# Sliding-window attention beside an S4 convolution: items of 512 queries by eight heads, square half tiles of the PE array, masks added by matmuls, the DFT split 64 by 32, and the order of the source

## The chip, the cores and the metric

The kernel runs on one core of a Trainium2 chip. A core has five engines that work side by side, each through its own instructions in order: PE (TensorE, matmuls; its weight loads are shown as PEld), DVE (VectorE), ACT (ScalarE), POOL (GpSimd) and SP (SyncE, which here only issues transfers). The metric is device time in microseconds of one execution; smaller is better.

PE is an array of 128 rows (the contraction) by 128 columns (the partitions of the output). A matmul may use only a part of it: 64 rows by 64 columns is called a half tile here, and four of them fill the array.

## The reference

Two independent parts share the launch, and their outputs stand side by side in a [1, 2048, 1152] tensor.

```python
# part A: attention, 32 heads of 18, each query sees the last 256 keys
qkv = (x @ wqkv).reshape(B, S, 3, H, Dh).transpose(2, 0, 3, 1, 4)   # S=2048, D=576
scores = einsum("bhqd,bhkd->bhqk", q, k) * Dh ** -0.5
mask = (i - j >= 0) & (i - j < 256)
p = softmax(where(mask, scores, -1e9))
a = einsum("bhqk,bhkd->bhqd", p, v).transpose(0, 2, 1, 3).reshape(B, S, D) @ wo
# part B: S4, 128 states per channel
K = einsum("dn,dnl,dn->dl", C, exp(dt * A * l), dt * B).real          # l = 0..2047
y = irfft(rfft(u, 4096) * rfft(K, 4096))[:2048] + u * Dskip
```

## The kernel before

The work stands in four stages.

*Projection, tables, first DFT of u.* `proj` (L153) splits x and wqkv into f16 high and low halves and forms q, k and v with 14 matmuls per output tile (`mm14`, L143); q and k go to DRAM as `qd`, v as `vd`. `tables` builds the S4 kernel K from exponentials, sines and cosines: products on POOL (L350), contraction over the 128 states in PE's four column groups (L388). `s1_u` (L433 and around) does the first step of a DFT of u. The three are generators, taken in turn by `merge` in fixed proportions; the framework's scheduler then orders the instructions of each engine by its own estimate of what is ready.

*First DFT of K* (`s1_k`): 48 matmuls, evacuated by ACT and DVE in turn (`evac`, L111), written to DRAM as `gk` in rows of 144 f32.

*The loop over 16 items.* An item is 1024 queries (half of them all) of 4 heads.
- `gmax` finds each query's largest score. The item's q is copied into a block-diagonal form of 4 heads by 32 queries (L580, DVE); a matmul gives the scores of 32 queries of 4 heads with their 288 keys (L593), a second adds the mask (L596), DVE takes the maximum (L602). The maxima are transposed, scaled to f16 and sent into a row of the stacked Q by four small transfers in POOL's queue (L613), so that the second score matmul subtracts them.
- `att_chunk` makes transposed scores of 128 keys by up to 384 queries from stacked f16 halves (L634), takes exponentials into SBUF (L636, ACT), cuts the two triangles out with `affine_select` on POOL (L645), and multiplies with V and a column of ones (L652), one head to each column group of 32.
- `norm` sends the sums through DRAM and back (den, rd, rb, all in POOL's queue), multiplies, splits the output in f16 halves, and stores it as `od`.
- `conv` runs beside it: 16 rounds of second DFT of x and K (L464), complex products on DVE (L486 to L495), inverse (L497), a store as `h`; then 16 rounds of the last inverse step (L517), an addition of u x Dskip (L513, L519) and the store of the output.
- `wo` is the output projection (again `mm14`); `wo_load` (L685) fetches and splits its weights through one tile named raw, in two rounds of four loads.

PSUM's eight banks are given out by use: two for the maxima's S, two for the scores ST, one for po, three for everything else (fps). `merge` mixes item i's `att_unit` (weight 23), the next item's `gmax` (17), `conv` (7) and from item 9 on `wo` (3), and the scheduler orders the rest, so that for instance wo_load's work lies beside the end of the projection.

*The end*: what is left of conv's last step, and the output projection of the second half.

## Time and profile before

| | |
|---|---|
| median of 3 runs | 1373.83 us (1372.09 to 1378.88) |
| span of the profiled execution, first to last instruction | 1366.8 us |
| the profiled execution's own time | not listed apart from its span; the median lies 7.0 us above that |
| busy: PE, DVE, ACT, POOL | 74%, 55%, 44%, 40% |
| granted clock of PE, mean | 0.828 |
| moved by transfers | 162.34 MB, 119 GB/s on average |

A row of groups reads: line of the code, engine, operation, output<-input by the program's names, their shapes, how many; behind the bar the busy time in us and the mean ns of one; behind the next bar the time that the engine sat idle just before them, and who ended that idle time. A row of the timeline reads: start in us, length in us, engine, line, operation, tiles, shape and count, and in brackets the idle time before it. An f32 matmul is recorded as two. PE's records include the way through the array, so that two may overlap; "issue" is time in which the engine waited for nothing that the profile shows. The clock is a share of full speed.

### The profile page before, as it was taken

How to read it: one execution, taken by the hardware profiler on the slowest of the kernel's cores; microseconds unless marked ns; L12 is line 12 of the kernel's file. 1: busy time of each engine (PE TensorE's matmuls, PEld its weight loads, DVE VectorE, ACT ScalarE, POOL GpSimd, SP SyncE). 2: the span in 40 equal slices, each digit the busy share in tenths (PEclk: the TensorE clock that was granted, in tenths of full speed). 3: DMA queues.
4: the chain of work that ended last, by engine and by line, in shares of the span. 5: the costliest groups of instructions: out<-in, count | busy, mean ns of one | idle time of the engine just before them, and what ended most of it. 6: DMA issues, size and time to landing. Idle time of an engine off the chain costs nothing.

```text
span 1366.8 us, 25524 instructions
## 1 busy us (share of the span) xinstructions
PE 1009.0 (74%) x10314; PEld 535.1 (39%) x10314; DVE 755.2 (55%) x1229; ACT 599.5 (44%) x879; POOL 549.1 (40%) x700
## 2 busy tenths in 40 slices
PE   1548898798889864876797789667888896666338
PEld 1224464464455532333343334333444453222116
DVE  4797667777753254566766677544555765411210
ACT  2867687687783320432343234422443352233002
POOL 0024343454450260244543354333534454576640
PEclk8659999999999986788888888757999997776559
DMA  9563142133125668144433444225344423434673
GB/s 269 141 181 103 34 116 75 54 75 98 50 56 153 168 179 229 52 128 113 125 117 107 127 125 146 84 65 143 87 114 137 140 75 109 105 88 118 160 177 130
DMA packets 155541, 162.34 MB, mean 119 GB/s; under 512 B 34752, under 2 KB 128512, under 8 KB 155232
## 3 DMA queue, kind: packets, MB, share of 16 engines
q1 hardware_dynamic: 138768, 128.65, 33.9%
q0 software_dynamic: 15152, 28.08, 7.2%
q10 hardware_dynamic: 1504, 3.99, 1.0%
q8 instruction: 81, 1.33, 0.4%
q14 instruction: 36, 0.29, 0.1%
HBM read 103.11 MB, written 57.15 MB: 117 GB/s over the span
## 4 chain that ended last, share of the span: by engine, by line
PE 43%; DVE 22%; DMA 14%; ACT 9%; issue 6%; POOL 5%; SPq 2%; ACTq 0%; DVEq 0%; POOLq 0%
PE po L652 7%; PE ST L634 6%; PE fps L464 5%; PE S L593 5%; PE pp L151 5%; DVE m L602 4%; DMA Q<-m 4%; PE fps L151 4%; ACT P L636 3%; PE fps L497 3%; PE kp L388 2%; PE pp L431 2%; DMA den<-osb 2%; DMA gk<-g 2%; DVE Qbd L580 2%
## 5 line engine op out<-in xcount | busy, mean ns | idle before, releaser
L636 ACT ACTIVATE P<-ST,esc 128x1024 f32<-128x1024 f32 (+1 forms) x192 | 203.5, 1060 | 270.3 <-PE ST L634 242.6
L602 DVE TENSOR_REDUCE m<-S 128x2 f32<-128x576 f32 x224 | 168.7, 753 | 163.1 <-PE S L596 161.4
L645 POOL TENSOR_SCALAR_AFFINE_SELECT P<-P 128x512 f32<-128x512 f32 x240 | 159.7, 695 | 199.5 <-ACT P L636 189.2
L350 POOL TENSOR_TENSOR m<-A,tr 128x1024 f32<-128x1024 f32 x72 | 149.5, 2098 | 193.5 <-PE kp L388 143.9
L593 PE MATMUL S<-kh,Qbd 96*128 96x288 f16 (+7 forms) x512 | 135.4, 323 | 87.4 <-DVE m L602 55.3
L634 PE MATMUL ST<-Q,K 96*128 96x384 f16 (+2 forms) x704 | 141.3, 320 | 65.4 <-ACT P L636 38.1
L652 PE MATMUL po<-P,V 128*32 128x256 f32 (+2 forms) x1408 | 132.9, 458 | 14.3 <-POOL P L645 13.1
L634 PEld LDWEIGHTS <-K 96*128 96x128 f16 x704 | 64.8, 108 | 150.5 <-issue 132.3
L388 PE MATMUL kp<-Q,m 128*32 128x64 f32 x4608 | 87.6, 229 | 27.5 <-DVE Q L371 10.5
L388 PEld LDWEIGHTS kp<-Q,m 128*32 128x32 f32 x4608 | 74.6, 115 | 55.6 <-issue 41.8
L593 PEld LDWEIGHTS <-Qbd 96*128 96x128 f16 x512 | 56.3, 111 | 97.1 <-issue 38.3
L596 PE MATMUL S<-bias,idb 128*128 128x64 bf16 x448 | 92.0, 216 | 0.0
L431 PE MATMUL pp<-ut,w 128*128 128x288 f32 x128 | 51.4, 526 | 42.2 <-DMA ut<-in_u_dram 24.9
L652 PEld LDWEIGHTS po<-P,V 128*32 128x32 f32 x1408 | 41.4, 122 | 82.1 <-issue 42.9
L596 PEld LDWEIGHTS <-idb 128*128 128x128 bf16 x448 | 47.9, 108 | 62.3 <-issue 59.3
L464 PE MATMUL fps<-tx,w 128*64 128x288 f32 x256 | 66.1, 456 | 0.0
L497 PE MATMUL fps<-Y,i 128*128 128x288 f32 x128 | 56.1, 537 | 11.1 <-DVE Y L495 6.3
L464 PE MATMUL fps<-tk,w 128*64 128x288 f32 x256 | 61.4, 430 | 0.4 <-DVE t L487 0.4
L517 PE MATMUL fps<-ho,i 128*64 128x288 f32 x128 | 29.7, 593 | 39.7 <-DMA ho<-h 33.3
L519 DVE TENSOR_TENSOR tk<-fps,tx 128x288 f32<-128x288 f32 x32 | 14.4, 457 | 73.6 <-PE fps L517 65.6
L114 ACT ACTIVATE X<-fps 128x288 f32<-128x288 f32 x64 | 25.8, 409 | 66.5 <-PE fps L464 62.1
L114 ACT ACTIVATE g<-pp 128x288 f32<-128x288 f32 (+1 forms) x84 | 34.5, 446 | 46.1 <-PE pp L431 25.3
(160 smaller groups left out, 1918.8 us busy)
## 6 DMA issues: line engine op xcount, KB each, us to landing
gx<-g SPq DMA_DIRECT2D x32, 288.0 KB
qd<-qst SPq DMA_DIRECT2D x36, 256.0 KB
gk<-g SPq DMA_DIRECT2D x16, 576.0 KB
tx<-gx SPq DMA_DIRECT2D x16, 576.0 KB
tk<-gk SPq DMA_DIRECT2D x16, 576.0 KB
h<-ho POOLq DMA_DIRECT2D x16, 576.0 KB, 3.6
ho<-h SPq DMA_DIRECT2D x64, 144.0 KB
raw<-in_xT_dram SPq DMA_DIRECT2D x16, 512.0 KB
```

Source lines behind the costliest of these rows:

```text
L151: self.nc.tensor.matmul(ps, u, v, start=(i == 0), stop=(i == len(ops) - 1))
L350: self.nc.gpsimd.tensor_tensor(m, A[:, ch, a0:a0 + 8].unsqueeze(3).to_broadcast(sh), tr[:, ch, part, 0:8].unsqueeze(2).to_broadcast(sh), o ...
L388: nc.tensor.matmul(kp[32 * st:32 * st + 32, c % 2 * JJ2 + j, :], m[:, ch, a0:a0 + 32], Q[:, ch, term % 2, :], start=(term == 0), stop=(ter ...
L464: nc.tensor.matmul(ps[64 * par:64 * par + 64, :288], w2[:, par, 64 * part:64 * part + 64], t[:, 2 * hs:2 * hs + 2, par, :], start=True, st ...
L497: nc.tensor.matmul(ps[:, :288], i1[:, par, :], Y, start=True, stop=True)
L593: nc.tensor.matmul(ps[:, u, :n[u]], bdt[:, t].rearrange("p j q -> p (j q)"), kh[:, k0:k1], start=True, stop=False, skip_group_check=True)
L596: nc.tensor.matmul(ps[:, u, :288].rearrange("p (a b) -> p a b", b=32)[:, 0:9:8], self.idb, self.bias, start=False, stop=True, skip_group_c ...
L602: nc.vector.tensor_reduce(m[:, 2 * sp:2 * sp + 2], ps[:, :, :n[0]], axis=AX.X, op=OP.max)
L634: nc.tensor.matmul(ps[:, u, o:o + n], d["K"][:, j, k0:k0 + 128], d["Q"][:, j, q0:q0 + n], start=True, stop=True, skip_group_check=True)
L636: nc.scalar.activation(pt[:, 2 * jp:2 * jp + 2, lo:hi], ps[:, :, lo:hi], AF.Exp, scale=self.esc)
L645: nc.gpsimd.affine_select(v, v, pattern=[[0, 4], [sg, 128]], compare_op=OP.is_ge, fill=0.0, base=-1 if far else 0, channel_multiplier=-sg)
L652: nc.tensor.matmul(po[32 * j:32 * j + 32, t0 * 128:t1 * 128], d["V"][:, kb * 76 + 19 * j:kb * 76 + 19 * j + 32], P[off // 512][:, j, o:o + ...
```

## The change

*Items.* An item is 512 queries of 8 heads: chunk c of four, octet o of four. The eight heads are four pairs; the two heads of a pair lie in partitions 0 to 63 and 64 to 127 of Q and K, each with its 54 rows of f16 halves. Q, K and V come from DRAM in the layout of the item (`qq`, `kk`, `k0`, `vd`), with each head's queries in a row. Three sets of Q and K are kept, and `load` fetches two items ahead.

*Half tiles.* The maxima (`smax`) and the scores (`att`) are made by four matmuls of 64 rows by 64 columns at a time, two heads of two pairs, into two banks: head r of pair-half b writes partitions 64 (r ^ b) and on of bank b. Blocks are 64 keys by up to 320 queries, so that less lies outside the window. P times V uses tiles of 64 rows by 32 columns, eight at a time. The block-diagonal copy of Q is gone.

*Masks.* POOL's affine_select is gone. Four further matmuls per piece, identity by a table of 0 and -3e38, add the mask to the scores in PSUM before the exponential.

*DFT.* 2048 is split into 64 by 32 where it was 32 by 64. Tiles in the first step have 64 rows (u) or 32 rows (K), in the second 64 rows by 32 columns, in the inverse 32 rows by 64 columns. There are 8 rounds of 3 thirds of the channels; ACT evacuates the spectrum of x, DVE multiplies it with that of K in PSUM by two wide products, POOL forms the sums Y. Dskip is added to K's first tap, so that u isn't read a second time. What goes to DRAM is written in rows of 2304 or 4608 bytes.

*PSUM and order.* In the loop three pairs of banks, "ring", serve maxima, scores, DFT and output projection in turn, and the fourth pair is po. The scheduler is off there (`manual_schedule`): each engine's instructions stand in the order of the source, written out as 16 items of five steps. `norm` is a generator that goes one part a step; its transfers, the maxima's and h's move from POOL's queue to SP's, so that SP issues all of them. `wo_load` stands behind the fifth step of the first item, `wo` gets a step from item 5 on and works on a chunk of 512 queries once its four items are normalised.

The diff, cut ("..." stands for lines left out):

```diff
-HQ = 1024
-HK = HQ + 256
+CQ = 512
+CK = 768
...
+def s1_u(self):
...
+    for ch in range(16):
+        ut = self.p["s1u"].tile([128, D], F32, name="ut")
+        for r in range(2):
+            nc.sync.dma_start(ut[64 * r:64 * r + 64], uv[:, (16 * r + ch) * D:(16 * r + ch + 1) * D])
...
+        for k in range(2):
+            ps = [self.p["pps"].tile([128, 512], F32, name="pp")[:, :288] for _ in range(2)]
+            for r in range(2):
+                nc.tensor.matmul(ps[r], self.wu[64 * r:64 * r + 64], ut[64 * r:64 * r + 64, 288 * k:288 * k + 288],
+                                 start=True, stop=True)
+            for r in range(2):
...
+def s1_k(self):
...
+    for n in range(16):
...
+            for h in range(2):
+                for u in range(2):
+                    s = 2 * q + u
+                    b = 32 * h + 2 * n
+                    nc.tensor.matmul(ps[:, u, :288], self.wk[32 * s:32 * s + 32, h],
+                                     self.K[32 * s:32 * s + 32, b:b + 2].rearrange("p l j -> p (l j)"),
+                                     start=(h == 0), stop=(h == 1), skip_group_check=True)
...
+        nc.sync.dma_start(gv[:, 2 * n * D:2 * n * D + 2 * D], st.rearrange("p l s j -> p (l s j)"))
+        yield
+def slot(self):
+    return self.p["ring"].tile([128, 2, 512], F32, name="ring")
...
+def spectra(self, t, ch):
...
+    px, pk = self.slot(), self.slot()
+    for x, ps in ((tx, px), (tk, pk)):
+        for i in range(2):
+            for q in range(2):
+                for s in range(2):
+                    for r in range(2):
+                        b = 2 * q + (r ^ s)
+                        o = (2 * s + q) * 64 + 32 * i
+                        nc.tensor.matmul(ps[32 * b:32 * b + 32, s, 192 * i:192 * i + 192],
+                                         w2[64 * r:64 * r + 64, o:o + 32],
+                                         x[64 * r:64 * r + 64, 2 * s + q, 192 * ch:192 * ch + 192],
+                                         start=(i == 0), stop=True, skip_group_check=True)
+    v = lambda z: z[:, :, :384].rearrange("p s (i j) -> p s i j", i=2)
+    X = fy.tile([128, 2, 2, 192], F32, name="X")
...
+    nc.scalar.activation(X, v(px), AF.Copy)
...
+    tt(t1, X, v(pk)[:, :, 0:1].to_broadcast(sh), op=OP.mult)
+    tt(t2, X, v(pk)[:, :, 1:2].to_broadcast(sh), op=OP.mult)
...
+    nc.gpsimd.tensor_tensor(Y[:, 0], t1[:, :, 0], t2[:, :, 1], op=OP.subtract)
+    nc.gpsimd.tensor_tensor(Y[:, 1], t1[:, :, 1], t2[:, :, 0], op=OP.add)
+    return Y
+def inverse(self, t, ch, Y):
...
+    ps = self.slot()
+    for s in range(2):
+        for i in range(2):
+            for b in range(4):
+                o = (2 * s + i) * 64
+                nc.tensor.matmul(ps[64 * (b % 2):64 * (b % 2) + 64, b // 2, 192 * s:192 * s + 192],
+                                 i1[32 * b:32 * b + 32, o:o + 64], Y[32 * b:32 * b + 32, i, s],
+                                 start=(s == 0 and i == 0), stop=(i == 1), skip_group_check=True)
+    nc.scalar.activation(self.ho[:, :, :, 192 * ch:192 * ch + 192].rearrange("p s b j -> p b s j"),
+                         ps[:, :, :384].rearrange("p b (s j) -> p b s j", s=2), AF.Copy)
...
+def conv(self):
...
+    for t in range(8):
+        for ch in range(3):
+            if ch == 1 and t < 7:
+                self.conv_load(t + 1)
+            Y = self.spectra(t, ch)
+            yield
+            if late is not None:
+                self.inverse(*late)
+            late = (t, ch, Y)
+            yield
...
+def smax(self, i):
...
+    for qb in range(8):
+        k0 = max(64 * qb, 256 if c == 0 else 0)
+        k1 = 64 * qb + 320
+        n = k1 - k0
+        full = n == 320
+        for pp in range(2):
+            ps = self.slot()
+            for b in range(2):
+                for r in range(2):
+                    z = 64 * (r ^ b)
+                    rr = slice(64 * r, 64 * r + 54)
+                    nc.tensor.matmul(ps[z:z + 64, b, :n], d["Q"][rr, 2 * b + pp, 64 * qb:64 * qb + 64],
+                                     d["k"][rr, 2 * b + pp, k0 - d["kc"]:k1 - d["kc"]], start=True, stop=False, skip_group_check=True)
+            for b in range(2):
+                for r in range(2):
+                    z = 64 * (r ^ b)
+                    rr = slice(64 * r, 64 * r + 64)
+                    if full:
...
+            nc.vector.tensor_reduce(mv[:, :, 8 * pp + qb], ps[:, :, :n], axis=AX.X, op=OP.max)
...
+    for b in range(2):
+        src = m16[16 * b:16 * b + 16].rearrange("s (h x) -> h s x", h=2)
+        for r in range(2):
+            nc.sync.dma_start(q[r:r + 1, 1024 * b:1024 * b + 1024].rearrange("o (s x) -> o s x", x=64), src[r ^ b])
+    yield
+def att(self, i):
...
+    def pv(P, bl):
+        for rel, o, q0, w in bl:
+            kb = rel + 4
+            for p in range(4):
+                for z in range(2):
+                    nc.tensor.matmul(po[32 * p:32 * p + 32, z, q0:q0 + w],
+                                     d["V"][64 * z:64 * z + 64, kb * 76 + 19 * p:kb * 76 + 19 * p + 32],
+                                     P[p % 2][64 * z:64 * z + 64, p // 2, o:o + w], start=(p, z) not in first,
+                                     stop=False, skip_group_check=True)
...
+    for n in (2, 4, 0, 1, 3):
+        bl = self.blocks(n, c)
+        P = []
+        for pp in range(2):
+            ps = self.slot()
...
+            for k, (rel, off, q0, w) in enumerate(bl):
+                for b in range(2):
+                    for r in range(2):
+                        z = 64 * (r ^ b)
+                        rr = slice(64 * r, 64 * r + 55)
+                        kc = 64 * (rel + 4) - d["kc"]
+                        nc.tensor.matmul(ps[z:z + 64, b, off:off + w], d["k"][rr, 2 * b + pp, kc:kc + 64],
+                                         d["Q"][rr, 2 * b + pp, q0:q0 + w], start=(k == 0), stop=False,
+                                         skip_group_check=True)
+            for blk, kinds in self.masks(bl):
+                w = 64 * len(kinds)
+                for b in range(2):
+                    for r in range(2):
+                        z = 64 * (r ^ b)
+                        rr = slice(64 * r, 64 * r + 64)
+                        nc.tensor.matmul(ps[z:z + 64, b, 64 * blk:64 * blk + w], self.idb[rr],
+                                         self.tm[rr, self.MO[kinds]:self.MO[kinds] + w], start=False, stop=True,
+                                         skip_group_check=True)
+            P.append(self.p["P"].tile([128, 2, 512], F32, name="P"))
+            nc.scalar.activation(P[pp][:, :, lo:hi], ps[:, :, lo:hi], AF.Exp, scale=self.esc)
+            yield
+        if pend is not None:
+            pv(*pend)
+        pend = (P, bl)
+        yield
+    pv(*pend)
+    osb = self.p["o"].tile([128, 2, 512], F32, name="osb")
+    nc.scalar.activation(osb, po, AF.Copy)
...
-                nc.gpsimd.affine_select(v, v, pattern=[[0, 4], [sg, 128]], compare_op=OP.is_ge, fill=0.0,
...
+def norm(self, i):
...
+    yield
+    nc.vector.reciprocal(den, den)
...
+    nc.gpsimd.tensor_tensor(osb, osb, rb, op=OP.mult)
+    yield
...
+    nc.gpsimd.tensor_tensor(h[:, 1], osb, h[:, 0], op=OP.subtract)
...
+def wo(self):
...
+    for c in range(4):
+        while self.done < 4 * c + 3:
+            yield
...
+            ps = self.slot()
+            for h in range(2):
+                self.mm14(ps[:, h, :288], (self.woh, self.wol), (oh, ol), slice(h * 288, h * 288 + 288),
+                          slice(t * 128, t * 128 + 128), flip=True)
+                if h == 0:
+                    yield
+            nc.scalar.activation(y, ps[:, :, :288], AF.Copy, scale=self.osc)
...
+for n, b, s in (("fs", 2, None), ("ho", 1, None), ("fy", 2, None), ("att", 1, None), ("m", 2, None),
+                ("P", 4, None), ("v", 3, None), ("o", 2, None), ("n", 1, None), ("wo", 1, None),
+                ("wo2", 1, None), ("ring", 3, PSUM), ("po", 1, PSUM)):
+    self.pool(e1, n, b, s)
+e1.enter_context(self.tc.manual_schedule())
+self.att_setup()
+self.osb, self.done = {}, -1
+self.load(0)
+self.load(1)
+def chain(f):
+    for i in range(16):
+        yield from f(i)
+def step(g, n=1):
+    for _ in range(n):
+        next(g, None)
+sm, conv, wo = chain(self.smax), self.conv(), self.wo()
+step(sm, 20)
+norms = []
+k = 0
+for i in range(16):
+    at = self.att(i)
+    for s in range(5):
+        step(at, 2)
+        step(sm)
+        step(at)
+        step(sm, 2)
+        if (4 * k + 4) // 5 > (4 * k) // 5:
+            step(conv)
+        if s == 2:
+            step(sm)
+        for g in list(norms):
+            if next(g, 0) == 0:
+                norms.remove(g)
+        if i >= 5:
+            step(wo)
+        if s == 1 and i < 14:
+            self.load(i + 2)
+        if s == 4 and i == 0:
+            self.wo_load()
+        k += 1
+    step(at)
+    norms.append(self.norm(i))
+for g in (*norms, conv, wo):
+    for _ in g:
+        pass
```

547 lines of the change are left out of this document (239 added, 308 removed).

## The prediction

> **What bounds the kernel now.** I read the page first, then the busy time of each engine by stage, then the groups by line, then single stretches of the timeline.
>
> ```profile
> span 1366.8 us, 25524 instructions
> PE 1009.0 (74%) x10314; PEld 535.1 (39%) x10314; DVE 755.2 (55%) x1229; ACT 599.5 (44%) x879; POOL 549.1 (40%) x700
> ...
> PE 43%; DVE 22%; DMA 14%; ACT 9%; issue 6%; POOL 5%; SPq 2%; ACTq 0%; DVEq 0%; POOLq 0%
> ```
>
> The span is 1366.8 us; the median of the runs shown is 1373.83, so 7 us lie around the span. I make the sum against the span and add the 7. No engine is full: PE leads with 74%, and the chain that ended last passes through PE, VectorE, transfers, ScalarE and GpSimd in turn. Next the stages (projection, tables and first DFT of u; first DFT of K and the ramp; the loop over 16 attention items; the end). Columns: stretch, its length, then each engine's busy us.
>
> ```profile
> core 0: us, PE busy (x) PEld busy (x) DVE busy (x) ACT busy (x) POOL busy (x), PEclk, DMA share, GB/s
> 0.00:467.00 467.00, 350.89 (x5851) 210.86 (x5851) 308.00 (x433) 311.71 (x506) 152.71 (x82) 0.89 0.40 111
> 467.00:548.00 81.00, 49.36 (x174) 25.81 (x175) 36.03 (x50) 16.36 (x36) 31.54 (x14) 0.77 0.69 196
> 548.00:1277.00 729.00, 562.03 (x4003) 269.02 (x4001) 400.77 (x728) 262.35 (x320) 336.55 (x560) 0.82 0.40 111
> 1277.00:1367.00 90.00, 46.74 (x288) 29.40 (x288) 10.36 (x20) 9.06 (x17) 28.32 (x44) 0.67 0.53 151
> ```
>
> The loop takes 729 us, 45.6 us for an item of 1024 queries and 4 heads. In it PE is busy 562 us (with latencies counted), VectorE 401, GpSimd 337, ScalarE 262. So it is bound by handing work round with single PSUM buffers, not by one engine. What one pass costs, and what each group waited for:
>
> ```profile
> L636 ACT ACTIVATE P<-ST,esc 128x1024 f32<-128x1024 f32 (+1 forms) x192 | 203.5, 1060 | 270.3 <-PE ST L634 242.6 <-POOL P L645 15.3 <-PE po L652 9.7
> L602 DVE TENSOR_REDUCE m<-S 128x2 f32<-128x576 f32 x224 | 168.7, 753 | 163.1 <-PE S L596 161.4
> L645 POOL TENSOR_SCALAR_AFFINE_SELECT P<-P 128x512 f32<-128x512 f32 x240 | 159.7, 695 | 199.5 <-ACT P L636 189.2 <-issue 8.7 <-DVE Y L494 1.4
> L350 POOL TENSOR_TENSOR m<-A,tr 128x1024 f32<-128x1024 f32 x72 | 149.5, 2098 | 193.5 <-PE kp L388 143.9 <-DVE A L338 22.5 <-ACT qst L207 14.5
> ```
>
> The exponentials waited 243 us for the score matmuls, the maxima 161 us for theirs, GpSimd 189 us for the exponentials. That is a circle, and the change rebuilds it.
>
> **The change part by part.** An item becomes 512 queries of 8 heads, the same 16 x 4096 query-heads. Prices of PE first, from PE's timeline:
>
> ```profile
> 242.02 1.99 PE L388 MATMUL kp<-Q,m 128*32 128x64 f32 x128
> ...
> 645.63 0.30 PE L593 MATMUL S<-kh,Qbd 96*128 96x288 f16 x1
> 645.76 0.20 PE L596 MATMUL S<-bias,idb 128*128 128x64 bf16 x1
> 645.80 0.29 PE L593 MATMUL S<-kh,Qbd 96*128 96x288 f16 x1
> 645.92 0.19 PE L596 MATMUL S<-bias,idb 128*128 128x64 bf16 x1
> 646.04 0.71 PE L464 MATMUL fps<-tk,w 128*64 128x288 f32 x4
> ```
>
> An f16 matmul of 288 columns and a mask of 64 follow at 0.13 and 0.04 us: one column per 0.42 ns. The 128 f32 records of 64 columns in 1.99 us are 15.5 ns each, where one alone would hold the array for 64 x 2 / 2.4 = 53 ns: the four column groups run side by side, and an f32 matmul is two records of two cycles a column. From 645.92 to 646.04 a 64-column mask gives way to another array shape: 0.12 us against 0.04 for the same shape, so a change of shape costs about 0.09 us.
>
> Array time of a full item if all tiles of one shape run side by side, at 2.4 GHz: maxima 16 x (320 + 128 columns) 3.0 us; scores 2 x 2560 columns 2.1; added masks 2 x 1024 columns 0.9; P times V 2560 columns x 4 cycles 4.3; DFT of x and K, 1.5 x 32 matmuls x 192 x 4 / 8 tiles 1.9; inverse 1.0; last DFT step 1.0; output projection, 28 matmuls of 288 columns, 3.4. Sum 17.4 us; at the loop's granted clock of 0.82, 21; with some 22 changes of shape 23. The 296 loads of 64-column weights are bounded from above by the rows 645.63 to 645.92 (two 128-column loads in 0.16 us, so 0.04 each for 64): 11.8 us against 6 us of streaming, so at most 6 more. Whether the row halves run side by side no row of before shows; the column groups do, so I take it that they do, and price the other case as a rival.
>
> By the row at 242.02 four tiles give 53 / 15.5 = 3.4 times one. The Trainium skill, TensorE: Matmul & The Clock Gate, Part 3 (Measured speedup vs the span model), gives 3.07 for four row tiles. By that figure the packed 14 us become an estimated 18, by the row 16.5; either lies inside the waits that the walk below contains.
>
> ScalarE's and VectorE's prices beside those above:
>
> ```profile
> L114 ACT ACTIVATE X<-fps 128x288 f32<-128x288 f32 x64 | 25.8, 409 | 66.5 <-PE fps L464 62.1 <-DVE m L602 3.7
> ...
> L370 DVE TENSOR_TENSOR Q<-cs,mg 128x512 f32<-128x512 f32 x36 | 24.5, 682 | 26.5 <-PE kp L388 12.6 <-PE x L284 6.4 <-ACT cs L366 6.1
> ...
> L672 ACT ACTIVATE oh<-osb 128x1024 f16<-128x1024 f32 x16 | 16.8, 1052 | 32.2 <-DVE osb L670 32.2
> ...
> L486 DVE TENSOR_TENSOR t<-X,fps 128x288 f32<-128x288 f32 x32 | 14.5, 452 | 11.2 <-PE fps L464 10.5 <-ACT X L114 0.4
> ```
>
> ScalarE, per item: ten exponentials of 1024 columns x 1.1 (the 1060 ns is a mean with shorter ones) 11.0; the copy of the 1024-column output 1.1, which moves here from VectorE; 3 evacuations of 768 columns at 0.87 (between 288: 409 ns and 1024: 1052 ns) 2.6; the cast 1.05; output copies 1.2. Sum 17.0 us. VectorE: 16 maxima of 640 columns at 0.82 (753 ns for 576, plus 64 x 1.03) 13.1; 3 products of 768 columns at 0.95 (452 ns for 288, 682 for 512) 2.9; small ones 0.9. Sum 16.9 us; the block-diagonal copies (L580) are gone. GpSimd loses 160 us of masks (off ScalarE's path only in part: 15.3 us of its waits) and gets two normalisation passes of 2.1 us (row L350) and two Y sums an item: some 7.5 us, hidden. SP takes every transfer, about 32 an item at 0.4 to 0.6 us of issue, 13 to 19 us (rows at 431.18 and 432.15 below): also below 20. So three engines want 17 to 23 us per item. The order and the waits decide.
>
> They go round three PSUM pairs in the order of the source. The handover from these rows:
>
> ```profile
> 647.64 0.30 PE L593 MATMUL S<-kh,Qbd 96*128 96x288 f16 x1
> ...
> 647.93 0.19 PE L596 MATMUL S<-bias,idb 128*128 128x64 bf16 x1
> ...
> 648.16 0.76 DVE L602 TENSOR_REDUCE m<-S 128x2 f32<-128x576 f32 x1 [0.40 <-PE S L596]
> ...
> 648.97 0.28 PE L593 MATMUL S<-kh,Qbd 96*128 96x288 f16 x1 [0.63 <-DVE m L602]
> ...
> 651.00 0.60 PE L634 MATMUL ST<-Q,K 96*128 96x384 f16 x4 [0.34 <-ACT P L636]
> ...
> 651.63 1.12 ACT L636 ACTIVATE P<-ST,esc 128x1024 f32<-128x1024 f32 x1 [0.69 <-PE ST L634]
> ```
>
> The last mask starts 647.93, its reduction 648.16: 0.2 us after the stream. The reduction ends 648.92, PE starts 648.97: 0.05 us. The exponential starts 0.63 us after its first matmul (427 ns of columns, again 0.2). A score pair E thus holds its buffer 0.5 (512 columns, 200 of masks, 0.2) + 1.1 + 0.05 = 1.65 us, a maximum D 0.4 (448 columns, 0.2) + 0.82 + 0.05 = 1.27. The order of a step is E E D, PV, D D, then DFT pairs X K or an inverse I. By hand, each pair waiting for the release three before it: E 0, E 0.3, D 0.6; PV 0.8 to 1.75; D 1.75; D 2.78 (second exponential ends 2.72); X 2.97, K 3.65; the two products end 6.62. Next step: E 4.3, E 4.8, D 6.68 (K's buffer), PV to 7.85, D 7.85, D 8.05, I 8.25; the following E starts at 9.12. Two steps 9.1 us. Of five steps four carry DFT work: 18.2, one without 3.0, the sixteenth maximum 0.9, output copy and cast 1.5, output projection (which also holds one of the three buffers through a whole step) 3.4: 27.0, and 0.5 for the clock: 27.5 us for a full item. The four items of the first 512 queries have shorter keys: 3.1 us less of exponentials, 2.6 of maxima, no output projection: 18.5. Loop: 12 x 27.5 + 4 x 18.5 = 404 us, for 729.
>
> wo_load is a loss. The scheduler had put it beside the end of the projection; now it stands in the source's order behind the first item. Its rounds before:
>
> ```profile
> 425.16 0.37 SPq L121 DMA_DIRECT2D raw<-in_wo_dram  x1
> ...
> 431.18 0.37 SPq L121 DMA_DIRECT2D raw<-in_wo_dram  x1
> ...
> 432.15 0.59 SPq L123 DMA_DIRECT2D raw<-in_wo_dram  x1
> ```
>
> ```profile
> 430.24 0.90 DVE L695 TENSOR_REDUCE amxo<-raw 128x1 f32<-128x720 f32 x1 [0.83 <-ACT raw L694]
> ```
>
> One tile, so each load waits for the reduction before it: at 425.16 and at 431.18 a round starts, 6.0 us. Eight rounds now stand one behind another on SP, ScalarE and VectorE, with nothing between them, and PSUM drains nowhere: 8 x 5.6 = 45 us (a little less than 6.0, since the SP rows between are gone). PE and GpSimd only finish what they have.
>
> The first DFT. In u's part pairs of matmuls use the row halves; PE's order up to the projection's end is otherwise nearly the same.
>
> ```profile
> 430.91 2.39 PE L431 MATMUL pp<-ut,w 128*128 128x288 f32 x8
> ```
>
> Two such groups stand in the last stretch, where PE alone sets the pace; each loses 1.2 us, and 19 more store issues on SP are hidden behind PE: 467 becomes 464. K's part and the ramp took 81 us, with this in them (rates in 40 slices of 466 to 521 us, and a piece of the chain):
>
> ```profile
> GB/s 0 178 48 0 194 270 303 168 247 184 296 264 326 279 273 64 6 0 0 0 0 0 85 289 162 213 216 250 255 321 214 298 204 306 228 256 269 275 284 225
> ```
>
> ```profile
> 487.43 8.39 DVE Qbd L580 x2
> ```
>
> The transfers stood still while the first item's block-diagonal copy held VectorE, 8.4 us, and so the evacuations. That copy is gone; rows of 4608 bytes replace 576. 9.4 MB at 300 GB/s, high among the busy slices since rows are longer, are 32 us; PE's 128 matmuls need 15 to 31. Loads of the first two items fall between. Then 16 maxima (10.5 us on VectorE) and the transposed maxima's way to Q before the first score: 18. Together 50 for 81.
>
> The end, after the last exponential:
>
> ```profile
> rb<-rd POOLq DMA_DIRECT2D x64, 128.0 KB, 2.8
> ...
> od<-oh POOLq DMA_DIRECT2D x64, 72.0 KB, 2.4
> ...
> Q<-m POOLq DMA_DIRECT2D x64, 2.0 KB, 4.7
> den<-osb POOLq DMA_DIRECT2D x64, 4.0 KB, 6.5
> ```
>
> ```profile
> 1333.55 29.25 PE fps L151 x224
> ```
>
> P times V and copy 2.0; den 4 (6.5 in GpSimd's queue; not below rb's 2.8), reciprocal and rd 2, rb 2.8, product 2.1, cast 1.05, difference 2.1, od 2.4, loads 5, half of the 29.25 us of matmuls 14.6, last copy and store 3.2, issues 2: 43 us. It was 90, because the last DFT step also stood there; now that is done inside the loop.
>
> Sum: 464 + 50 + 404 + 45 + 43 = 1006 us of span, 1013 with the 7 around it.
>
> **The rivals.** *Half the tiles wait* (20 in 100). If tiles in different rows take turns where they write one bank, maxima, scores, masks and first DFT double: 3.0 + 3.0 + 1.9 = 7.9 us of PE per item. About 6.5 of it shows in a full item, since PE would then be at 28 of 34 us, and 4 in a short one: 404 + 78 + 16, total 1107. For it: no row here shows row tiles. Against: P times V writes two banks, and the column groups overlap perfectly. The Trainium skill, TensorEngine Tiling (Array Packing), Gotcha 1: PSUM Pressure, says that different row tiles cannot use one PSUM bank at the same time; in the maxima both diagonal quarters write one bank, in different partitions, and by that rule this rival is the result. No row here can test it.
>
> *The engines alone count* (10 in 100): the waits fill each other up, 21 us for a full item and 15 for a short one: 312 for 404, total 921. For it: 1.65 us / 3 buffers is below 0.6. Against: 243 us of waits in the row of L636 with the same in-order PE.
>
> *The ring goes one at a time* (11 in 100), the slower side. If PE, in source order, never gets ahead of the engine that drains, the cycles add: 10 x 1.65 + 17 x 1.27 + DFT 9.2 + projection 4.3 + last step 1.8 = 53.4 us an item, about 43 for a short one: 813, total 1422. It decides from 1.4 us per buffer on (48 us per item, 34.5 buffers). For it: with one buffer of each kind, maxima came every 2.0 us (645.63, 647.64). Against: three buffers and two engines that drain them.
>
> **How the numbers follow.** My case has 55 in 100 and spans 950 to 1075 (24 to 32 us per full item). With the rivals of 20, 10 and 11, 4 are left for sums between 1150 and 1365. The range 905 to 1190 leaves out the ring and some of the edges, about 18 in 100. About 0.5% is what a measurement here tells from no change: faster 0.88, same 0.01, slower 0.11.
>
> **What would show it.** The maxima's matmuls (L641) in fours that start within some 20 ns show side-by-side tiles; in twos, the first rival. A gap of some 45 us on ScalarE and VectorE behind the first item, ended by raw<-in_wo, shows wo_load. Steps of 4 to 5 us and ScalarE near 60% busy in the loop show the walk; PE waiting before every ring pair for the engine just fed shows the third rival. K's stage should move over 250 GB/s without a pause. I am wrong if SP's one queue stalls the transposed maxima (a wait for Q at each item's start), which I costed at nothing because they are issued over one step, 5 us, ahead.

## The result and the profile after

The changed kernel takes 1365.59 us (median of 20 runs, 1354.49 to 1372.76), the kernel before 1374.88 us beside it (20 runs, 1367.35 to 1391.54): 0.9928 of the time, 95% interval 0.9905 to 0.995. It is faster by 0.7%, where 1013 us were forecast. The profiled execution has a span of 1364.4 us. The page, in the parts shown for the kernel before:

```profile
span 1364.4 us, 36796 instructions
PE 844.7 (62%) x16426; PEld 500.2 (37%) x16426; DVE 554.0 (41%) x780; ACT 573.4 (42%) x797; POOL 287.8 (21%) x184
...
DMA 13%; PE 10%; SPq 4%; ACT 3%; issue 2%; DVE 1%; POOL 0%; POOLq 0%; ACTq 0%; DVEq 0%
DMA K<-kk 6%; DMA hp<-h 4%; PE ring L154 2%; ACT P L739 2%; PE po L706 2%; PE ring L506 1%; PE ring L641 1%; PE ring L576 1%; PE ring L726 1%; DMA tk<-gk 1%; PE ring L533 1%; SPq L755 1%; DMA Q<-qq 1%; SPq L542 1%; SPq L618 0%
```

Every engine does less than before: PE 845 us for 1009, VectorE 554 for 755, ScalarE 573 for 600, GpSimd 288 for 549. The time has hardly moved all the same. The chain that ended last can be followed back only to 902 us here, a third of the span (its shares add up to 33%), so it can't be set beside the chain of before share by share. Within that third transfers lead, 13% of the span for PE's 10%, and the first name is the load of K. The same stretches as before:

```profile
core 0: us, PE busy (x) PEld busy (x) DVE busy (x) ACT busy (x) POOL busy (x), PEclk, DMA share, GB/s
0.00:467.00 467.00, 347.79 (x5786) 196.47 (x5787) 291.19 (x418) 302.37 (x491) 152.48 (x81) 0.94 0.36 105
467.00:548.00 81.00, 49.97 (x512) 34.94 (x513) 16.70 (x29) 16.68 (x29) 16.07 (x8) 0.65 0.48 166
548.00:1277.00 729.00, 404.21 (x9482) 242.75 (x9472) 243.41 (x328) 230.29 (x250) 105.79 (x89) 0.74 0.38 114
1277.00:1367.00 90.00, 42.72 (x655) 26.07 (x655) 2.67 (x6) 24.09 (x27) 13.40 (x6) 0.77 0.39 115
```

In the 729 us of the third row PE is busy 404 us for 562, VectorE 243 for 401, GpSimd 106 for 337. The work was taken away as forecast; waits stand in its place. The groups of the loop (548 to 1307 us) that answer to those of before, maxima, exponentials and the maxima's matmuls:

```profile
L654 DVE TENSOR_REDUCE m<-ring 128x2 f32<-128x640 f32 (+2 forms) x236 | 183.7, 796 | 406.2 <-PE ring L649 377.1 <-PE ring L652 28.7
L739 ACT ACTIVATE P<-ring,esc 128x1024 f32<-128x1024 f32 (+2 forms) x159 | 159.7, 1058 | 88.3 <-PE ring L735 88.3
...
L641 PE MATMUL ring<-K,Q 54*64 54x320 f16 (+3 forms) x944 | 86.6, 349 | 249.2 <-DMA K<-kk 132.7 <-ACT P L739 55.7 <-DVE m L654 47.0
```

The maxima waited 406 us for PE, and PE, at the first matmul of a maximum, 133 us for a load of K that no row of before had shown late. (Another 46 of PE's 47 us behind VectorE are one wait, wo_load's.) One such wait, in the chain in order of time and in the DMA rates in 40 slices of 918 to 943 us:

```profile
918.02 0.27 DVE den L757
...
918.31 0.36 SPq L759
...
920.99 0.74 SPq L618
...
922.96 17.21 DMA K<-kk
940.17 0.14 issue
940.30 0.32 PE ring L641
```

```profile
DMA  0041521334969968111124011114311111111110
GB/s 0 14 71 59 79 66 52 111 118 102 191 185 324 226 151 216 33 52 56 59 118 164 39 59 49 49 49 164 108 32 49 59 49 49 51 53 55 43 40 3
```

PE stands still for the last stretch of a transfer of 17.2 us. SP issued it late, too: the loads stand in its queue behind the store of the reciprocals (L759), which had to wait for VectorE (L757); such waits at L759 add up to 33 us in the loop. Meanwhile the DMA engines are hardly used: most slices after 928 us show a tenth of the 16 engines busy and some 50 GB/s. The other pieces of this name on the chain last 15.8 to 17.0 us (at 974.94, 1019.15, 1070.61, 1115.86). The trace's packets say why: an item's load of K is four transfers, two of 36 partitions that take rows from two sources and two of 18 from one. Together they have 108 packets of 6144 bytes. The median packet takes 0.236 us, and in the twelve full loads (those from kk) the packets take 14.9 to 19.2 us from the first to the last. In the median load 1.9 packets are under way at a time, as if two of the 16 engines worked.

Two more of the signs that the prediction named. Four tiles of a maximum, in PE's timeline:

```profile
851.05 0.33 PE L641 MATMUL ring<-K,Q 54*64 54x320 f16 x4
851.21 0.23 PE L649 MATMUL ring<-sm,idb 64*64 64x128 bf16 x4
851.27 0.31 PE L641 MATMUL ring<-K,Q 54*64 54x320 f16 x4
851.41 0.23 PE L649 MATMUL ring<-sm,idb 64*64 64x128 bf16 x4
```

Four tiles of 320 columns start together and give way 0.14 us later (851.27 to 851.41), four masks of 128 columns 0.06 us later (851.21 to 851.27). One tile alone needs 320 x 0.42 ns = 0.133 us, at the prediction's price of a column. All four run side by side, the two that write different halves of one bank included. And wo_load, in ScalarE's timeline, its first round, its last, and the copy that follows:

```profile
583.25 0.80 ACT L785 ACTIVATE raw<-raw 128x720 f32<-128x720 f32 x1 [5.86 <-DMA raw<-in_wo_dram]
...
621.44 0.90 ACT L794 ACTIVATE woh<-raw,or 128x720 f16<-128x720 f32 x1 [4.44 <-DMA raw<-in_wo_dram]
622.24 1.00 ACT L747 ACTIVATE osb<-po 128x1024 f32<-128x1024 f32 x1
```

From the end of the work before it (577.4) to 622.2 that is 45 us, the number forecast for this gap.

### The profile page after: what moved, and what is told of

Read it like the earlier page. It is cut to its first block, busy times and chain, and to the rows that moved or that the text cites. A ratio compares the mean times of both kernels' runs of the same rounds, so it can differ in the third digit from the quotient of the medians.

```text
span 1364.4 us, 36796 instructions
## 1 busy us (share of the span) xinstructions
PE 844.7 (62%) x16426; PEld 500.2 (37%) x16426; DVE 554.0 (41%) x780; ACT 573.4 (42%) x797; POOL 287.8 (21%) x184
## 5 line engine op out<-in xcount | busy, mean ns | idle before, releaser
L654 DVE TENSOR_REDUCE m<-ring 128x2 f32<-128x640 f32 (+4 forms) x256 | 194.1, 780 | 407.2 <-PE ring L649 377.1
L641 PE MATMUL ring<-K,Q 54*64 54x320 f16 (+4 forms) x1024 | 94.1, 350 | 255.3 <-DMA K<-kk 132.7
L739 ACT ACTIVATE P<-ring,esc 128x1024 f32<-128x1024 f32 (+2 forms) x160 | 160.7, 1058 | 88.3 <-PE ring L735 88.3
L641 PEld LDWEIGHTS <-Q 54*64 54x64 f16 x1024 | 46.3, 117 | 302.2 <-issue 297.7
L706 PE MATMUL po<-P,V 64*32 64x320 f32 (+4 forms) x2816 | 101.2, 409 | 0.6 <-issue 0.3
L450 PE MATMUL pp<-ut,wu 64*128 64x288 f32 x128 | 48.0, 602 | 44.1 <-DMA ut<-in_u_dram 18.7
L726 PE MATMUL ring<-Q,K 55*64 55x320 f16 (+4 forms) x1408 | 68.8, 293 | 7.7 <-ACT P L739 2.6
L649 PE MATMUL ring<-sm,idb 64*64 64x128 bf16 x896 | 62.1, 244 | 0.0
L154 PE MATMUL pp<-xh,wh 128*128 128x512 f16 x180 | 48.6, 393 | 2.3 <-DVE xh L205 1.9
L154 PE MATMUL pp<-xh,wl 128*128 128x512 f16 x180 | 48.0, 391 | 0.0
```

Source lines behind the costliest of these rows:

```text
L154: self.nc.tensor.matmul(ps, u, v, start=(i == 0), stop=(i == len(ops) - 1))
L450: nc.tensor.matmul(ps[r], self.wu[64 * r:64 * r + 64], ut[64 * r:64 * r + 64, 288 * k:288 * k + 288], start=True, stop=True)
L641: nc.tensor.matmul(ps[z:z + 64, b, :n], d["Q"][rr, 2 * b + pp, 64 * qb:64 * qb + 64], d["k"][rr, 2 * b + pp, k0 - d["kc"]:k1 - d["kc"]], s ...
L649: nc.tensor.matmul(out, self.idb[rr], self.sm[rr], start=False, stop=True, skip_group_check=True)
L654: nc.vector.tensor_reduce(mv[:, :, 8 * pp + qb], ps[:, :, :n], axis=AX.X, op=OP.max)
L706: nc.tensor.matmul(po[32 * p:32 * p + 32, z, q0:q0 + w], d["V"][64 * z:64 * z + 64, kb * 76 + 19 * p:kb * 76 + 19 * p + 32], P[p % 2][64 * ...
```

## The experiments

The theory after the result (A): transfers whose outermost dimension is two sources run on two DMA engines; K takes 17 us that way, is issued too short a time ahead, and what else falls on those two engines waits too. (In the ten items whose maxima stood at a load from kk, its first transfer was issued 2.6 to 15.2 us before PE ran out of work, in six of them under 5 us.) Rivals: (B) the ring, one pair at a time, sets the pace and the wait for K is its slack; (C) SP's one queue; later (D) in-order engines that stand at a late transfer with ring work behind them. Times are medians; the ratio is to the kernel before, run beside each.

| run | edit | us | ratio, 95% interval |
|---|---|---|---|
| changed kernel | | 1365.6 | 0.9928, 0.9905 to 0.995 |
| e1_split | K and Q by 18 partitions | 1225.6 | 0.889, 0.882 to 0.896 |
| e12_inter | order of rows alone | 1223.9 | 0.890, 0.881 to 0.899 |
| e2_early | loads issued earlier | 1351.0 | 0.981, 0.974 to 0.988 |
| e3_wo | wo spread over items | 1344.7 | 0.978, 0.970 to 0.985 |
| e4_all | e1, e2 and e3 | 1201.7 | 0.873, 0.867 to 0.880 |
| e5_norm | e4, normalisation spread | 1184.6 | 0.861, 0.858 to 0.864 |
| e6_pool | e4, its transfers on GpSimd | 1171.7 | 0.852, 0.848 to 0.857 |
| e7_oh | e5, earlier oh loads | 1166.4 | 0.848, 0.845 to 0.852 |
| e8_np | e7 and e6 | 1130.8 | 0.823, 0.818 to 0.829 |
| e9_best | e8, first pass of wo moved | 1099.9 | 0.803, 0.795 to 0.811 |
| e10_nold | no K, Q, V loads, items 7 to 15 | 1238.3 | 0.901, 0.895 to 0.908 |
| e11_walk | e9 and e10 | 1087.2 | 0.790, 0.784 to 0.796 |

**The form of the transfers (e1_split).**

```
-    nc.sync.dma_start(dv[64 * h + 18:64 * h + 54], src[0:1].to_broadcast([2, 18, 4 * n]))
+    nc.sync.dma_start(dv[64 * h + 18:64 * h + 36], src[0])
+    nc.sync.dma_start(dv[64 * h + 36:64 * h + 54], src[0])
...
-    nc.sync.dma_start(dv[64 * h:64 * h + 36], src)
+    nc.sync.dma_start(dv[64 * h:64 * h + 18], src[0])
+    nc.sync.dma_start(dv[64 * h + 18:64 * h + 36], src[1])
     nc.sync.dma_start(dv[64 * h + 36:64 * h + 54], src[0])
```

> The loads of K and Q that take rows from two sources at once (36 partitions) are written as transfers of 18 partitions from one source, as the kernel before had them; four more transfers an item, nothing else. Theory A, narrow transfers: in the trace of the changed kernel the K load takes 16 to 17 us and moves on about two engines, and maxima wait for it. It should now take 3 to 6 us; the 133 us that the row of L641 puts down to K<-kk vanish, and with them part of the waits for hp, tk and rb behind the same two engines: about 1170 to 1240, 0.86 to 0.91 of the changed kernel. Rival B, the ring one pair at a time sets the pace and the waits for K are only where its slack shows: 1330 or more. Rival C, SP's single queue is the limit: 64 more issues of 0.4 to 0.6 us make it slower, 1365 to 1400.

1225.6 us, 140 us less than the changed kernel, inside theory A's numbers. The 108 packets of a K load now take 5.1 to 7.2 us, 7.5 at a time; the group of the maxima's matmuls in e1_split:

```profile
L643 PE MATMUL ring<-K,Q 54*64 54x320 f16 (+2 forms) x920 | 81.0, 336 | 147.0 <-ACT P L741 55.0 <-DVE m L656 46.4 <-DMA K<-kk 39.0
```

The wait for K fell from 132.7 to 39.0 us, not to nothing. (The groups of e1_split and e12_inter are taken from 548 to 1200 us.) B, which gave 1330 or more, is out, and so is C in the form it was given: more issues on SP did not make the kernel slower.

**The form alone (e12_inter).** e1_split also made more and smaller transfers. Here the rows of the two sources lie interleaved, so that the source's outermost dimension is 18 rows, with two sources inside it.

```
-    nc.sync.dma_start(dv[64 * h:64 * h + 18], src[1])
-    nc.sync.dma_start(dv[64 * h + 18:64 * h + 54], src[0:1].to_broadcast([2, 18, 4 * n]))
+    nc.sync.dma_start(dv[64 * h + 36:64 * h + 54], src[1])
+    nc.sync.dma_start(dv[64 * h:64 * h + 36],
+                      src[0:1].to_broadcast([2, 18, 4 * n]).rearrange("a p n -> p a n"))
...
-    nc.sync.dma_start(dv[64 * h:64 * h + 36], src)
+    nc.sync.dma_start(dv[64 * h:64 * h + 36], src.rearrange("a p n -> p a n"))
```

> The changed kernel with the same four transfers for Q and four for K in an item, the same bytes in the same packets; only the rows of the two sources lie interleaved in the 36 partitions (row i of the one, row i of the other), so that the outermost dimension of the source is 18 long instead of 2. e1_split changed both the form and the number and size of the transfers; this changes the form alone. If the outermost dimension decides on how many engines a transfer runs (the Trainium skill, DMA: Bandwidth & Descriptors, Why a DMA increments its semaphore by 16 and not by 1, would give it nine for two): as e1_split or a little better, since SP issues four fewer, 1205 to 1235. If it was the size of the transfers or their number in flight: 1340 to 1370.

1223.9 us: the order of two dimensions is the whole of e1_split's gain. The same 108 packets of a K load take 4.9 to 7.9 us, 6.6 at a time, for 14.9 to 19.2 us and 1.9 at a time; the median packet takes the same (0.245 for 0.236 us). The group of the maxima's matmuls, and a K load on the chain of e12_inter:

```profile
L642 PE MATMUL ring<-K,Q 54*64 54x320 f16 (+2 forms) x920 | 82.7, 347 | 140.8 <-ACT P L740 55.8 <-DVE m L655 49.1 <-DMA K<-kk 23.7
```

```profile
966.33 5.62 DMA K<-kk
```

The Trainium skill, DMA: Bandwidth & Descriptors, section Why a DMA increments its semaphore by 16 and not by 1, says that a transfer is given the largest number of engines up to 16 that divides the outermost dimension of both sides, and on these queues the lowest-numbered ones. By that rule an outer 2 gives two engines and an outer 18 nine. The packets agree, with 1.9 at a time for the one and 6.6 and 7.5 for the other (each the median over twelve loads of a load's mean, its ends included). The traces don't name the engines, so which ones they were no run here shows.

**An earlier issue (e2_early).**

```
     at = self.att(i)
+    if i < 14:
+        self.load(i + 2)
     for s in range(5):
...
-        if s == 1 and i < 14:
-            self.load(i + 2)
```

> The load of item i+2 is issued ahead of item i's first step instead of in its second step, some 5 to 8 us earlier; its form stays. Theory A (narrow transfers, 17 us on two engines, against a lead of about 12 us): the wait for K shrinks by the 5 to 8 us in each of 14 items, 70 to 110 us less: 1255 to 1295; waits for hp and tk stay. If the two engines were full all the time (more bytes than they can move in an item) an earlier issue would bring nothing: 1350 to 1370. Rival B (ring): 1350 to 1370. Rival C (SP's queue): Q and K stand ahead of the row of the denominators, whose wait then moves the normalisation later: no gain, 1360 to 1390.

1351.0 us, 15 us less, where A gave 70 to 110. By the number alone this is what the expectation gave to engines that are always full (1350 to 1370). But no wait for K is left at the maxima in e2_early, although a full load's packets still take 15.2 to 17.5 us, so the lead was mended. (The lead in the expectation, about 12 us, was itself too long, by the 2.6 to 15.2 us above.) Its list of waits between 548 and 1307 us has a new one (total in us, how often, the longest), and the chain shows how it comes about:

```profile
DVE den L757 <- DMA den<-osb: 147.4, 14, 15.7
```

```profile
914.32 16.18 DMA V<-vd
930.52 1.93 DMA den<-osb
932.57 0.35 DVE den L757
932.92 0.69 DVE m L654
933.62 0.14 issue
933.75 2.84 PE ring L533 x32
```

V is a transfer of 128 partitions, yet it takes 16 us behind the narrow ones; the row of denominators is landed behind it, VectorE stands at their reciprocal, the next maximum behind that, PE behind the maximum. The wait did not go, it was passed on from PE to VectorE: the part of the expectation under C, that the denominators would be late, came true. Lead alone doesn't mend a slow transfer in a shared queue.

**wo_load (e3_wo).** wo_load becomes a generator with a yield behind each round's load, stepped in items 0 to 4.

```
+            yield
             nc.scalar.activation(t, t, AF.Abs)
...
+            yield
             nc.scalar.activation(self.woh[:, :, cs], t, AF.Copy, scale=self.so)
...
-        if s == 4 and i == 0:
-            self.wo_load()
+        if i < 5 and (i or s == 4):
+            step(wl)
```

> The eight rounds that load and split wo go one to a step through items 0 to 4 instead of all behind item 0. Theory (prediction): the stall of 45 us from 577 to 622 goes and nothing takes its place but some 1 us of work in a step: 1322 to 1332. Rival: the stall gave the loads of item 2 their time, and 10 to 17 us of it come back as a wait for K: 1332 to 1345. Rival: the rounds block SP ahead of other transfers: 1345 or more.

1344.7 us, 21 us less: item 0 ends 42 us earlier (its output copy at 580.2 for 622.2), and items 1 and 2 then take 57 us each where they had taken 39 and 48. That is the first rival's size, 24 us less than the gap of 45. What came back is in part wo's own waits (e9_best, below); how much of it is the loads that the stall had given time, these two runs don't separate.

**All three (e4_all).**

> All three edits. Theory A: the loop comes down to the walk of the prediction, 404 us with its first DFT-free start, so 475 + 70 + 404 + 60 for the end: 1010 to 1080. Rival B (ring): with waits for K and wo gone the ring still takes 40 us or more an item: 1250 to 1300. Rival C (SP's queue): the waits move to SP's other transfers (rb, the transposed maxima): 1150 to 1250.

1201.7 us, far above A's 1010 to 1080 and inside C's numbers. B is out, since items 6 to 8, full ones, took 33 to 37 us where it gave 40 or more. But the waits are not those that C named, rb and the transposed maxima. VectorE's and SP's timelines in e4_all show another:

```profile
823.67 0.95 DVE L517 TENSOR_TENSOR t<-X,ring 128x768 f32<-128x768 f32 x1
828.79 0.35 DVE L759 RECIPROCAL den<-den 128x32 f32<-128x32 f32 x1 [4.17 <-DMA den<-osb]
829.06 2.22 DVE L656 TENSOR_REDUCE m<-ring 128x2 f32<-128x640 f32 x3
```

```profile
818.52 0.26 SPq L619 DMA_DIRECT2D K<-kk  x1
...
820.99 0.35 SPq L625 DMA_DIRECT2D V<-vd  x1
821.44 1.62 SPq L774 DMA_DIRECT2D od<-oh  x4
824.01 3.08 SPq L757 DMA_DIRECT2D den<-osb  x4
```

Three maxima follow without a gap, so VectorE had work, and it stands 4.2 us at a reciprocal whose row SP issues only at 824 to 827, behind the loads and the stores. This is what theory D says.

**Steps between a transfer and its use (e5_norm, e7_oh) and the other queue (e6_pool, e8_np).** e5_norm puts one more yield ahead of the reciprocal, the row broadcast, the product and the cast in norm; e7_oh puts three more between the loads of oh and their matmuls; e6_pool and e8_np issue norm's transfers from GpSimd.

```
     yield
+    yield
     nc.vector.reciprocal(den, den)
...
     nc.sync.dma_start(oh[64 * i + 32 * z:64 * i + 32 * z + 32, 4], self.od[c, 256:288, i, z])
-    yield
+    for _ in range(4):
+        yield
...
-    nc.sync.dma_start(den[32 * p:32 * p + 32], ...)
+    nc.gpsimd.dma_start(den[32 * p:32 * p + 32], ...)
```

> On top of the three edits of e4_all (1202 us), the normalisation of an item gets one step more between a transfer and the instruction that waits for it: reciprocal, row broadcast, product and cast each one step later. Theory D: what is left of the gap to the walk is an in-order engine that waits for a transfer with ring work behind it (in e4_all VectorE stands 4 us at the reciprocal for den, ScalarE at the cast behind rb); 12 to 14 items lose 4 to 8 us each: 1100 to 1150. Rival B (ring): the ring's own handing over takes 33 us an item and the waits lie beside it: 1190 to 1205. Rival E: the longer normalisation holds its single buffers and the next item's waits for them: 1200 or more.

> On top of the three edits of e4_all, the normalisation's transfers (den, rd, rb, od) are issued from GpSimd's queue, as before the change, without further steps. If SP's one queue is what delays them (den stood behind the loads and stores issued ahead of it), den and rb come 2 to 5 us earlier and SP has 13 transfers an item less: 1130 to 1180. If the waits are those of the transfers themselves (6.5 us for den from GpSimd's queue in the kernel before): 1190 to 1215. Issuing on GpSimd holds its products: 1215 or more would show that.

> e5_norm, and the loads of the output projection (oh and ol) get three steps more before the matmuls that use them. In e4_all PE waits some 10 us for them once in four items, three times in the loop. Theory D: 25 to 30 us less than e5_norm. Rival: PE's stall is covered by the engines that catch up: less than 10 us.

> e7_oh (1166 us) with the normalisation's transfers issued from GpSimd's queue, as in e6_pool, where this brought 30 us against e4_all. If SP's queue and the longer way of the normalisation cost independently of each other: 1130 to 1145. If the extra steps had already hidden the lateness: 1160 to 1170.

e5_norm took 1184.6 us, 17 less than e4_all, where D gave 50 to 100; the number lies in none of the ranges given. VectorE's waits for den within the loop fell from 38 us (nine) to 16 (five), so one step was not always enough behind SP. e7_oh takes another 18 us off, between the 25 to 30 of D and the under 10 of its rival. e6_pool, without a step more, took 1171.7, 30 less than e4_all; e8_np, both, 1130.8, 36 less than e7_oh. The two add up. So part of the queue's cost was there after all (C), shown here for the normalisation. For K it isn't separated: the chain above has SP waiting at L759 with the loads behind it, and e2_early, which issues them ahead of that store, changes their lead in one with it.

**The rest of wo (e9_best).** In e7_oh items 1 and 2 took 46 us each. VectorE's and GpSimd's timelines there:

```profile
597.33 0.16 DVE L134 TENSOR_REDUCE om<-amxo 128x1 f32<-128x4 f32 x1
605.26 0.15 DVE L136 TENSOR_SCALAR og<-og 128x1 f32<-128x1 f32 x1 [7.77 <-POOL og L135]
```

```profile
604.85 0.38 POOL L135 PARTITION_ALL_REDUCE og<-om  x1 [6.24 <-issue]
```

The scale of wo is a maximum over all partitions, on GpSimd; VectorE, with the maxima of attention behind it, waits 7.8 us for it. Most of this lies ahead of the reduction's own record of 0.38 us: GpSimd stands 6.24 us put down to issue, and 5.8 to 5.9 us in e3_wo, e4_all, e5_norm and e8_np, where it also comes straight from other work. In the changed kernel, where GpSimd had been idle 25 us, VectorE waited only 0.55 us. What GpSimd does in these 6 us the trace doesn't say. e9_best does the first pass with its reduction during the first DFT of K (as wo_scale) and leaves the four rounds that split wo, with a step more behind each load, in items 0 to 3:

```
-            for _ in self.s1_k():
-                pass
+            ws = self.wo_scale()
+            for _ in self.s1_k():
+                next(ws, None)
```

> e8_np, with the first pass over wo (the four rounds that find its maximum, and the reduction over partitions on GpSimd, behind which VectorE stood 7.8 us in e7_oh) moved into the first DFT of K; only the four rounds that split wo stay in items 0 to 3. In e7_oh items 1 and 2 took 46 us each, against 25 to 33 us for items 3 and 4. If the wo rounds are the cause, 20 to 35 us less than e8_np; if it is the loads behind them (tx and tk, K of the first full item), less than 10.

1099.9 us, 31 less than e8_np; items 1 and 2 now take 25 and 33 us. This version beats both kernels: 0.803 of the time before. Its stretches, the loop cut at its own first and last exponential:

```profile
0.00:475.00 475.00, 355.29 (x5831) 201.62 (x5832) 295.65 (x428) 303.84 (x494) 152.99 (x82) 0.94 0.36 108
475.00:533.00 58.00, 39.65 (x466) 27.95 (x467) 16.70 (x29) 15.46 (x26) 16.12 (x9) 0.78 0.64 223
533.00:1034.00 501.00, 376.54 (x9939) 235.26 (x9939) 240.51 (x321) 242.68 (x263) 202.31 (x272) 0.91 0.58 171
1034.00:1096.00 62.00, 24.32 (x212) 15.98 (x196) 0.99 (x2) 8.72 (x11) 21.99 (x30) 0.69 0.31 99
```

**Without the loads (e10_nold, e11_walk).**

```
-    for nm, z, seq in (("Q", self.qq, (1, 0, 0)), ("K", self.kk, (0, 1, 0))):
+    for nm, z, seq in () if i >= 7 else (("Q", self.qq, (1, 0, 0)), ("K", self.kk, (0, 1, 0))):
...
+    if i >= 7:
+        return
```

> The changed kernel, but items 7 to 15 load no K, Q and V and use again what items 4 to 6 loaded (so the output is that of other keys and queries; all instructions of the engines stay). This takes the whole cost of these loads away, for nine of sixteen items. Theory A: those nine items go from 49 us each to 31 to 36, that is 115 to 160 us less: 1205 to 1250. Rival B (ring): less than 40 us, 1325 or more. Beside e1_split it also tells what the loads still cost with 18 partitions each: e1_split brought about 10 us an item.

> e9_best without the loads of K, Q and V in items 7 to 15. What is left of the transfers is off the ring or stands well ahead of its use. If the walk of the prediction (27.5 us for a full item) is right, the items from 7 on take 26 to 30 us and the whole 30 to 60 us less than e9_best. If the ring needs more than I walked, they stay at 33 us or more and the total within 20 us of e9_best.

e10_nold took 1238.3 us, 127 us less for nine loads left out, inside A's numbers. An item's load is waited for within the second item before it; items 5 to 13 together take 326.5 us for 453.5 (from output copy to output copy), 14 us less each. e12_inter, with the loads, has 362.8: the order of rows alone gives 91 of these 127 us back. e11_walk took 1087.2, only 13 us less than e9_best, in what the expectation gave to a longer ring. The items lie on both sides of its 33 us: 25.9, 27.6 and 29.1 where the output projection doesn't run (items 9, 4, 5), 28.4 in item 13 with the last DFT step alone, 36.4 twice with the projection running throughout (7, 11), 42.1 in item 12, where PE stands 9.0 and 2.6 us for hp, the last DFT step's loads. Most of a quiet item of e11_walk (item 4) on ScalarE:

```profile
656.06 2.11 ACT L744 ACTIVATE P<-ring,esc 128x1024 f32<-128x1024 f32 x2
659.03 2.12 ACT L744 ACTIVATE P<-ring,esc 128x1024 f32<-128x1024 f32 x2 [0.86 <-PE ring L740]
663.76 0.81 ACT L512 ACTIVATE X<-ring 128x768 f32<-128x768 f32 x1 [2.60 <-PE ring L506]
664.87 2.12 ACT L744 ACTIVATE P<-ring,esc 128x1024 f32<-128x1024 f32 x2 [0.30 <-PE ring L740]
669.49 0.81 ACT L536 ACTIVATE ho<-ring 128x768 f32<-128x768 f32 x1 [2.50 <-PE ring L533]
670.19 2.12 ACT L744 ACTIVATE P<-ring,esc 128x1024 f32<-128x1024 f32 x2
...
677.02 2.11 ACT L744 ACTIVATE P<-ring,esc 128x1024 f32<-128x1024 f32 x2
```

The pairs of exponentials start 3.0, 5.8, 5.3 and 6.8 us apart (the last with the normalisation's cast of 1.05 us in it). A step without DFT takes the 3.0 us walked; those with it 5.3 to 5.8, where I walked 4.3 and 4.8.

## Why the prediction was right and wrong

The direction was right, the size was not: the span is 1364 us for 1006, and the time lies outside the range. That the time fell at all is no merit of the reasoning, since what was saved and what was lost came out nearly equal. By the prediction's own boundaries (first and last exponential at 548.1 and 1307.3):

| term | forecast | measured | difference |
|---|---|---|---|
| to the end of the projection | 464 | 475 | +11 |
| first DFT of K, ramp | 50 | 73 | +23 |
| loop with wo_load | 404 + 45 | 759 | +310 |
| end | 43 | 57 | +14 |

**Array prices, wo_load: right but for one.** Row tiles run side by side (0.14 us for four of 320 columns), so the first rival falls, and with it the rule of the Trainium skill, TensorEngine Tiling (Array Packing), Gotcha 1: PSUM Pressure, as far as it was read to hold for two halves of one bank. The gap at wo_load was 45 us as forecast, though spreading it gave back only 21 (e3_wo). One array price was wrong. The 1.0 us an item of the inverse comes out with eight tiles at once, 0.64 us each time. Its sixteen matmuls, 32 records, start in fours, one four every 0.16 us, and from their start to PE's next matmul it is 1.46 us in the median of 24 (changed kernel, e9_best and e11_walk alike). The source pairs row group b with column half b % 2 only, so every four lies in the same four tiles and the other four are never used. That is 2.2 us an item for 1.0. Of VectorE's and ScalarE's busy times here the sum and mean over nine items of e9_best (two short, seven full), from the copy of item 1's output at 592 to that of item 10's at 874 us:

```profile
sum 282.00, PE 213.01 PEld 136.22 DVE 154.97 ACT 141.20 POOL 135.38; mean PE 23.67 PEld 15.14 DVE 17.22 ACT 15.69 POOL 15.04
```

Per item 17.2 us of VectorE and 15.7 of ScalarE, for the 16.9 and 17.0 worked out. GpSimd has 15.0 here, where it issues the normalisation's transfers as well; in four items of the changed kernel (858 to 1051 us) it has 8.2, for 7.5.

**The step that failed: "SP takes every transfer, about 32 an item at 0.4 to 0.6 us of issue, 13 to 19 us ... also below 20".** Transfers were costed by their issue alone, and everything else about them at nothing. No term asked how long a load takes to land in its new form, how far ahead of its use it is issued, what it shares its engines with, and which in-order engine stands at it. The new loads' outer dimension of two was in the diff; the kernel before loaded 18 partitions from one source. The price is shown: e12_inter changes that form alone and takes 142 us off. The sign I named for being wrong, a wait for Q and its transposed maxima behind SP's queue, is not what came: PE waited for K, at the first maxima of an item. In the loop's terms, 759 us became 629 in e12_inter, 130 us for the form of the loads, and 501 in e9_best, 128 us more, in which the forecast 45 of wo_load are contained; 97 stay above the walk's 404.

**Second part of the same step: engines that wait in order.** With the loads mended, e9_best is 124 us faster than e12_inter, by edits that only move waits away from the ring or transfers off SP (it has e1_split's form of the loads, which takes the same time). I had called the normalisation hidden because GpSimd does it, and had not followed its reciprocal on VectorE and its cast on ScalarE, both with ring work behind them. The added waits were counted by the engine that does the work, not by what queues behind them.

**The walk: mis-sized.** 27.5 us for a full item was near for quiet items (25.9 to 29.1 us without the projection, where the walk without its 3.4 has 24.1), and the twelve full items of e9_best average 32. Short items were not short: e9_best's first four take 117 us together, 43 more than 4 x 18.5. I subtracted exponentials and maxima from the sum, but their steps carry the same DFT pairs, and it is these steps that came out longer; wo's four splitting rounds lie there too. In the item of e11_walk shown above, the step of 5.3 us has the inverse, 1.46 us for the 0.64 counted. In the step of 5.8 us P times V takes 1.9 us, from 660.06 to 661.95, at a granted clock of 0.50 (659.5 to 662.5 us), where the next step's takes 1.03 us, at 666.35; the walk had 0.5 us an item for the clock. ScalarE was busy 32% of the loop, 48% in e9_best, for the near 60% named. The third rival, 53 us an item, is refuted by the same items.

**The ends.** The first maximum stands at 533.6 us; in e12_inter at 520.3. So at least 13 of the 23 us on K's part belong to the narrow loads, between the stores of the first DFT; from 475 to 515 us 199 GB/s were moved, with stretches near 50, and 267 in e12_inter, for the 250 without a pause that I named. The rest of it stays open, as do the 11 us of the projection's stage: it ends at 477 us in e9_best too, and no run separated its parts. At the end I had 2 us for issues; on the chain of the changed kernel the last denominators are issued 10 us after the last exponential, behind item 14's normalisation, and the issues of den, rb, od and oh add some 7 us.

## What to carry to other kernels

A diff that rearranges loads is read for each transfer's outermost dimension, its landing time in the new form and its lead, before any array time is counted; if two sources go into one tile, interleave the rows so that the long dimension is outside. In a schedule written out by hand, ask of each wait on a transfer what stands behind it on that engine and ahead of it in its queue: mending one wait without the other (e2_early) only hands it on. And busy times that fall together with an unchanged span are the sign to leave the engines' busy rows and read the waits and the chain.

## What the runs showed that I had not expected

- The same bytes of K in the same four transfers and the same 6144-byte packets take 14.9 to 19.2 us or 4.9 to 7.9, by the order of two dimensions alone.
- Narrow transfers slow wide ones: V, over 128 partitions, stands 16.2 us on the chain behind K's in e2_early, and 5.6 to 6.5 us in the chain of e4_all, where K is spread over more engines.
- The reduction over partitions on GpSimd kept VectorE waiting 7.8 us (e7_oh) though its own record lasts 0.38 us: some 6 us pass on GpSimd ahead of it.
- Thirty-two rows by 64 columns leave room for eight tiles, but the inverse uses only four of them, 1.46 us for 0.64: the diff shows it (output half b % 2 for row group b), and its starts on PE, in fours 0.16 us apart, fit that.
